# Second layer's first product by Strassen's seven block products over 768 tokens, its d_ff sums in SBUF, its weights unpacked early to DRAM

## The chip, the cores and the metric

The kernel runs on one core of one Trainium2 chip. The core has a matmul engine (TensorE: PE, and PEld for its weight loads), VectorE (DVE), ScalarE (ACT), GpSimd (POOL) and SyncE (SP), which here issues the DMAs. Each engine takes its instructions in the order written for it; semaphores hold it where it needs another's result. The metric is the device time of one execution in microseconds.

## The reference, cut to what matters

```python
x = attention(q, k, v, f)             # 4 x 8 x 576 x 64, causal with decay -> 2304 tokens x 512
h = x @ w_in                          # layer 1: 512 -> 2048
g = s * np.maximum(h, 0.0) ** 2 + b
x = g @ w_out                         # 2048 -> 512
h = x @ w_in                          # layer 2, other weights: 512 -> 2048
g = np.maximum(h, 0.0) + alpha * np.minimum(h, 0.0)
return g @ w_out                      # 2048 -> 512, float32
```

## The kernel before

**Number format.** Each factor of a product is split into two parts of reduced precision, `hi` and `lo = x - hi`, and each product takes three passes (hi·hi, lo·hi, hi·lo, the tuple `PASSES`). So a block product of 512 (d_model) by 128 (d_ff) by 512 tokens is 4 × 3 = 12 matmuls of 512 columns.

**Who sets the order.** Operations are put down as tasks (`task`) with a modelled cost, what they read and write, the ring buffers they use and a priority; a list scheduler in the kernel file writes each engine's instructions from these. A task offered for two engines goes where the model finishes it first. On the chip each engine then follows its list in order.

**Stages.** Attention writes x; beside it layer 1's first d_ff half runs over six blocks of 256 tokens. From about 398 us on come the remaining tokens (groups `67` and `8`, 512 and 256 tokens) and then layer 1's second half for the groups p0, p1 and p2 of 512 tokens. Layer 2 follows at 597 us over groups of 512, 512, 512, 512 and 256 tokens (`order = [3, 0, 1, 2, 4]`).

**One step of layer 2** (`moe_step` with `moe` 2), for one chunk `fc` of 128 of the 2048 d_ff: the first product `t_mm1` (L851, 12 matmuls into a PSUM bank of ring h or k); ACT scales it by alpha (L858); DVE takes the larger of that and the plain value (L864); ACT casts to `hi` (L868); DVE subtracts to `lo` (L879); the second product `t_mm2` (L886, 12 matmuls, each 512 output columns wide) adds into four PSUM banks of rings a and b, which sum over all 16 chunks. `finish_out` then copies the four banks to SBUF (L982) and stores them.

**Between the layers.** `finish_x1` adds layer 1's first-half sums, kept in DRAM (`pa_d`), to the banks of its second half (L953), splits the result into hi and lo, and stores it (`x1_d`); `load_x` brings it back.

**Weights.** They come as 64-bit words. `convert` loads one 128 × 512 block (512 KB, `raw`), scales words on ACT (L426), puts them together in three DVE operations (L417, L420, L423; the last two read both `raw` and the half-made `cv`), then casts to hi on ACT and takes lo on POOL (L443; for `wo2` on DVE, L441). Layer 2's are converted partly during layer 1, partly after it has begun.

## Time and profile before

| | before |
|---|---|
| time, median of 3 runs | 1008.03 us |
| runs | 1007.60, 1008.03, 1010.24 us |
| span of the profiled execution | 1006.3 us |
| its own time | not listed apart from the runs |
| busy share of PE, DVE, ACT, POOL | 99%, 55%, 45%, 23% |

The span runs from the first to the last instruction that the profile shows. An engine's busy time is the sum of its instructions' durations, register, branch and DMA-issuing ones left out; PE's matmuls overlap a little at their ends, so that the pace of a run of equal matmuls (start to start) is shorter than the listed mean of one.

### The profile page before, as it was taken

How to read it: one execution, taken by the hardware profiler on the slowest of the kernel's cores; microseconds unless marked ns; L12 is line 12 of the kernel's file. 1: busy time of each engine (PE TensorE's matmuls, PEld its weight loads, DVE VectorE, ACT ScalarE, POOL GpSimd, SP SyncE). 2: the span in 40 equal slices, each digit the busy share in tenths (PEclk: the TensorE clock that was granted, in tenths of full speed). 3: DMA queues.
4: the chain of work that ended last, by engine and by line, in shares of the span. 5: the costliest groups of instructions: out<-in, count | busy, mean ns of one | idle time of the engine just before them, and what ended most of it. 6: DMA issues, size and time to landing. Idle time of an engine off the chain costs nothing.

```text
span 1006.3 us, 15579 instructions
## 1 busy us (share of the span) xinstructions
PE 996.9 (99%) x5691; PEld 835.1 (83%) x5691; DVE 554.0 (55%) x1262; ACT 450.7 (45%) x1067; POOL 234.1 (23%) x275
## 2 busy tenths in 40 slices
...
GB/s 221 234 191 171 139 110 210 83 104 131 136 116 31 189 142 131 138 132 259 100 172 68 219 224 175 1 0 126 1 1 84 42 1 0 84 1 1 1 42 21
DMA packets 45519, 106.45 MB, mean 106 GB/s; under 512 B 4492, under 2 KB 23524, under 8 KB 44516
## 3 DMA queue, kind: packets, MB, share of 16 engines
...
q8 instruction: 45, 0.74, 0.3%
...
## 4 chain that ended last, share of the span: by engine, by line
PE 96%; DVE 1%; ACT 1%; issue 0%; DMA 0%; POOL 0%; SPq 0%; POOLq 0%; ACTq 0%
PE h L851 24%; PE k L851 16%; PE b L886 11%; PE a L888 9%; PE b L891 9%; PE a L886 9%; PE t L802 5%; PE t L749 4%; PE a L891 2%; PE s L674 2%; PE s L675 2%; PE s L679 2%; PE h L392 1%; DMA ft<-in_f_dram 0%; DVE cv L423 0%
## 5 line engine op out<-in xcount | busy, mean ns | idle before, releaser
L851 PE MATMUL h<-x,i 128*128 128x256 f32 (+1 forms) x1344 | 256.6, 340 | 0.6 <-DVE r L862 0.6
L851 PEld LDWEIGHTS h<-x,i 128*128 128x128 f32 x1344 | 210.9, 189 | 32.3 <-DVE r L862 1.9
L851 PE MATMUL k<-x,i 128*128 128x512 f32 (+1 forms) x672 | 153.4, 377 | 0.0
L851 PEld LDWEIGHTS k<-x,i 128*128 128x128 f32 x672 | 120.7, 188 | 25.5
L886 PE MATMUL b<-o,g 128*128 128x512 f32 x480 | 121.1, 393 | 0.0
L879 DVE TENSOR_TENSOR g<-r,g 128x512 fp32r<-128x512 f32 (+1 forms) x80 | 51.1, 638 | 120.9 <-ACT g L868 120.9
L709 POOL TENSOR_SCALAR e<-e,rec 128x128 f32<-128x128 f32 (+4 forms) x144 | 88.7, 627 | 86.1 <-DVE rec L702 35.7
L886 PEld LDWEIGHTS b<-o,g 128*128 128x128 f32 x480 | 90.2, 188 | 20.5
L868 ACT CAST g<-r 128x512 fp32r<-128x512 f32 (+1 forms) x78 | 45.1, 578 | 137.1 <-PE b L886 87.2
L888 PE MATMUL a<-g,o 128*128 128x256 f32 x768 | 104.5, 285 | 0.0
L443 POOL TENSOR_TENSOR i<-cv,i 128x512 fp32r<-128x512 f32 x32 | 47.7, 1490 | 243.5 <-ACT i L433 235.8
L886 PE MATMUL a<-o,g 128*128 128x512 f32 x384 | 98.8, 393 | 0.0
L888 PEld LDWEIGHTS a<-g,o 128*128 128x128 f32 x768 | 96.8, 190 | 1.2 <-issue 0.7
L891 PE MATMUL b<-g,o 128*128 128x512 f32 x384 | 95.3, 394 | 0.0
L877 DVE SCALAR_TENSOR_TENSOR g<-r,small,g 128x256 fp32r<-128x256 f32 (+1 forms) x104 | 70.1, 674 | 41.4 <-ACT g L870 40.7
L698 ACT ACTIVATE e<-e,ngm 128x128 f32<-128x128 f32 (+4 forms) x144 | 84.2, 586 | 14.8 <-DVE ngm L693 12.9
L891 PEld LDWEIGHTS b<-g,o 128*128 128x128 f32 x384 | 72.0, 188 | 16.8
L886 PEld LDWEIGHTS a<-o,g 128*128 128x128 f32 x384 | 71.1, 188 | 15.1
L870 ACT ACTIVATE g<-r,small 128x256 fp32r<-128x256 f32 (+1 forms) x90 | 53.2, 591 | 59.9 <-PE b L891 30.1
L693 DVE CUSTOM_DVE_ANT_0 e<-s,mask 128x128 f32<-128x128 f32 (+4 forms) x144 | 67.1, 480 | 16.9 <-PE s L675 7.8
L749 PE MATMUL t<-ident,e 128*128 128x128 f32 (+1 forms) x400 | 65.4, 276 | 3.5 <-ACT pt L758 2.1
L864 DVE SCALAR_TENSOR_TENSOR r<-k,sg_t,r 128x512 f32<-128x512 f32 (+1 forms) x40 | 27.9, 697 | 73.3 <-ACT r L858 73.3
...
## 6 DMA issues: line engine op xcount, KB each, us to landing
...
```

Of the source, the lines that this page charges most:

```text
L693: nc.vector.tensor_tensor_reduce(e.t[0:rows, k0:k1], st_.t[0:rows, 0:w], mask[0:rows, m0:m0 + w], -0.125 if u.f32 else -1.0, init, ALU.add ...
L698: nc.scalar.activation(x, x, AF.Exp, bias=ng[0:rows, col:col + 1], scale=-1.0, accum_out=sm[0:rows, col:col + 1])
L709: eng.tensor_scalar(x, x, rc[0:rows, col:col + 1], 1.0, ALU.mult, ALU.mult)
L749: nc.tensor.transpose(pp.t[0:kw, i * P:i * P + P], e.t[:, P * kb:P * kb + kw], ident)
L802: nc.tensor.matmul(o.t[64 * j:64 * j + 64, a - q0:z - q0], vb.t[0:kr, kb, j, :], uu.pt[jj].t[0:kr, kb * PTS + a:kb * PTS + z], start=(i == ...
L851: nc.tensor.matmul(ps.t[:, 0:w], wv[:, wl, kc, :], x.t[:, kc, xl, x0:x0 + w], start=(n == 0), stop=(n == 3 * KC - 1))
L870: eng.activation(g.t[:, 0, 0:w], r.t[:, 0:w], AF.Identity, bias=b_t)
L877: nc.vector.scalar_tensor_tensor(g.t[:, 1, 0:w], r.t[:, 0:w], b_t, h, ALU.add, ALU.subtract)
L879: nc.vector.tensor_tensor(g.t[:, 1, 0:w], r.t[:, 0:w], h, ALU.subtract)
L886: nc.tensor.matmul(acc[u].t, g.t[:, gl, u * P:u * P + P], wo.t[:, wl, :], start=(first and i == 0), stop=end)
L888: nc.tensor.matmul(acc[u // 2].t[:, T * (u % 2):T * (u % 2) + T], wo.t[:, wl, u * P:u * P + P], g.t[:, gl, 0:w], start=(first and i == 0 a ...
L891: nc.tensor.matmul(acc[u].t[:, 0:w], wo.t[:, wl, u * P:u * P + P], g.t[:, gl, 0:w], start=(first and i == 0), stop=end)
```

## The change

**First product.** Layer 2 goes over three groups of 768 tokens, and takes d_ff in eight pairs of chunks. For a pair, W (512 × 256) and x (512 × 768) are seen as 2 × 2 blocks (d_model halves by d_ff chunks, d_model halves by token halves). Winograd's form of Strassen's scheme gives the four 128 × 384 result blocks from seven block products of 256 × 128 by 384 tokens in place of eight. Each is 2 × 3 matmuls of 384 columns (L1096 of the new file). The table `PRODUCTS` names for each the weight operand, the token operand and the bank (Z, X, Y, W: one bank each of rings h and k, two of ring a); the last three add onto a product already there. Between them ACT copies two banks to SBUF (`s1`, `s5`, L1108) and DVE makes the sums (`u2`, `u3`, `c12`, `c21`, L1111, L1140; six of the 24 `u3` sums with two SBUF operands of the first group's pairs are POOL's, L1141).

**Gates.** Each of the four blocks gets the operations of before, on 384 columns (ACT L1124, DVE L1126, cast L1128, `lo` L1130).

**Second product and its sums.** Six tiles `y` of 128 tokens, each six matmuls of 512 columns over the pair's two chunks (L1162), in ring b of four banks; DVE adds each to a sum in SBUF (L1171; the first pair of a group copies, L1168), stored after the last pair.

**Token operands.** `finish_x2` takes the place of `finish_x1`: it makes the seven token operands of the scheme out of x's four blocks, with hi and lo of each, on DVE and ACT, through a ring `so` of four buffers, and stores them in 84 pieces (`x2_d`).

**Weights.** `keep` unpacks all 32 blocks of `wi2` and `wo2` during layer 1, and stores the unpacked float32 (`w2f_d`). `sums_of`, in the first group, makes four sums of weight blocks and hi and lo of all seven operands of a pair (on DVE, ACT and POOL), and stores them (`w2i_d`, 1.835 MB a pair), from where the other two groups load them (each group takes the pairs in the opposite direction to the one before, and its first two pairs' operands are still there); `outs_of` makes hi and lo of `wo2` for every pair and group anew. Pools for these (`w2`, `px`) open as layer 1's weights are done with. Attention and layer 1's first half keep their operations.

```diff
-    open_pool("wA", side="left")
+    open_pool("wA", side="right")
...
-    x1_d = [dram.tile([P, KC, 2, T2 if n < 4 else T], F32R, name=f"x1_d{n}") for n in range(5)]
+    x2_d = [dram.tile([P, 7, 2, 2, TH], F32R, name=f"x2_d{n}") for n in range(3)]
+    w2i_d = [dram.tile([P, 7, 2, T], F32R, name=f"w2i_d{n}") for n in range(NP2)]
+    w2f_d = {(key, n): dram.tile([P, 512], F32, name=f"{key}f_d{n}") for key in ("wi2", "wo2") for n in range(NF)}
...
+        "wi2": ring("w2", "wi2", 2, [P, 7, 2, T], F32R),
+        "wo2": ring("w2", "wo2", 2, [P, 2, 2, 512], F32R),
+        "cf": ring("w2", "cf", 4, [P, 512], F32),
+        "so": ring("w2", "so", 4, [P, 2 * T], F32),
+        "sw": ring("w2", "sw", 1, [P, 4, T], F32),
+        "y": ring("psc", "b", 4, [P, 512], F32),
+        "gq": ring("px", "gq", 8, [P, 2, TH], F32R),
+        "rt": ring("px", "rt", 2, [P, TH], F32),
...
+    def keep(key, fc, prio):
+        cv = R["cv"].buf()
+        K = unpack(key, fc, prio, cv)
+        task(("sp", kb_of(P * 2048), lambda: load(w2f_d[key, fc], cv.t.bitcast(F32))), r=[(K, "v")], w=[(K, "f")], bufs=[cv], prio=prio)
+
+    def fetch(key, fc, tag, prio):
+        c = R["cf"].buf()
+        K = (tag, key, fc)
+        task(("sp", kb_of(P * 2048), lambda: load(c.t, w2f_d[key, fc])), r=[((key, fc), "f"), "w2"], w=[K], bufs=[c], prio=prio)
+        return c, K
+
+    def sums_of(p, tag, prio):
...
+        both(T, [k1], [S[0]], [c1, sw], lambda e: e.tensor_tensor(s_of(0), part(c1, 0), part(c1, 1), ALU.add))
+        both(T, [k0, k1], [S[2]], [c0, c1, sw], lambda e: e.tensor_tensor(s_of(2), part(c0, 0), part(c1, 0), ALU.subtract))
+        both(T, [k0, S[0]], [S[1]], [c0, sw], lambda e: e.tensor_tensor(s_of(1), s_of(0), part(c0, 0), ALU.subtract))
+        both(T, [k0, S[1]], [S[3]], [c0, sw], lambda e: e.tensor_tensor(s_of(3), part(c0, 1), s_of(1), ALU.subtract))
+        done = []
...
+            task([("act", act(n, False), lambda a=a, z=z, src=src: nc.scalar.copy(wi.t[:, a:z, 0, :], src())),
+                  ("dvp", dve2(n), lambda a=a, z=z, src=src: nc.vector.tensor_copy(wi.t[:, a:z, 0, :], src()))], r=r, w=[hk], bufs=bufs + [wi], prio=prio)
+            both(n, r + [hk], [lk], bufs + [wi],
+                 lambda e, a=a, z=z, src=src: e.tensor_tensor(wi.t[:, a:z, 1, :], src(), wi.t[:, a:z, 0, :].bitcast(F32), ALU.subtract))
+            done += [hk, lk]
+        task(("sp", kb_of(P * 14336), lambda: rdma(w2i_d[p], wi.t)), r=done, w=[("w2i", p)], bufs=[wi], prio=prio)
+        return wi, done
...
+                def split(op, e, h, k=k, blk=blk, s0=s0, hw=hw, d0=d0, f=f, fk=fk, piece=piece):
...
+                    task(("sp", kb_of(P * 8 * hw), lambda: rdma(x2_d[blk][:, op, k, :, d0:d0 + hw], o2())), r=[(K, "hi"), (K, "lo")],
+                         w=[("x2d", blk, op, k, d0)], bufs=[st_], prio=epr)
...
+                split(0, 0, 0)
+                less(0, 0, 0, 1, 0, 0)
+                split(3, 0, 0)
+                split(2, 1, 1)
+                less(0, 1, 1, 1, 0, 1)
+                split(5, 0, 1)
+                less(1, 1, 1, 1, 0, 0)
+                split(4, 1, 1)
+                split(1, 1, 0)
+                less(1, 0, 1, 0, 1, 1)
+                split(6, 1, 0)
...
+    PRODUCTS = ((0, 0, "Z", True), (3, 3, "X", True), (5, 5, "Y", True), (4, 4, "W", True),
+                (1, 1, "Z", False), (6, 2, "X", False), (2, 6, "Y", False))
...
+                    if n == 0:
+                        wi, ki = sums_of(p, n, z - 8)
+                    else:
+                        wi, ki = R["wi2"].buf(), [("w2il", n, p)]
+                        task(("sp", kb_of(P * 14336), lambda wi=wi, p=p: rdma(wi.t, w2i_d[p])), r=[("w2i", p)], w=ki, bufs=[wi], prio=z - 6)
+                    wo, ko = outs_of(p, n, z - 6)
...
+        def product(i):
+            wop, xo, bk, start = PRODUCTS[i]
+            xb, view, slot = xop[xo]
...
+                for k in range(2):
+                    for wl, xl in PASSES:
+                        nc.tensor.matmul(b.t[:, 0:TH], wi.t[:, wop, wl, k * P:k * P + P], x[:, k, xl, :], start=(start and m == 0), stop=(m == 5),
+                                         skip_group_check=True)
...
+        for i in range(4):
+            product(i)
+            if i == 0:
+                copy("s1", "Z")
+            if i == 1:
+                copy("s5", "X")
+        add("u2", "W", "s1")
+        add("u3", "Y", "u2")
+        task([("dvp", dve(TH), lambda: nc.vector.tensor_tensor(t("u3"), t("u3"), t("s5"), ALU.add)),
+              ("pool", pool2(TH), lambda: nc.gpsimd.tensor_tensor(t("u3"), t("u3"), t("s5"), ALU.add))], r=[("t", "s5")], w=[("t", "u3")],
+             bufs=[tmp["u3"], tmp["s5"]], prio=epr)
+        gate(1, 1, src="u3")
+        product(4)
+        gate(0, 0, bankname="Z")
+        product(5)
+        add("c12", "X", "u2")
+        gate(0, 1, src="c12")
+        product(6)
+        add("c21", "Y", "u2")
+        gate(1, 0, src="c21")
+        for h in (1, 0):
+            for j in range(3):
+                u = 3 * h + j
+                y = R["y"].buf()
+                YK = (K, "y", u)
+
+                def go(h=h, j=j, y=y):
+                    m = 0
+                    for e in range(2):
+                        for gl, wl in ((0, 0), (0, 1), (1, 0)):
+                            nc.tensor.matmul(y.t, G[e, h].t[:, gl, j * P:j * P + P], wo.t[:, e, wl, :], start=(m == 0), stop=(m == 5))
+                            m += 1
+                task(("pe", 6 * MM[512], go), r=ko + [((K, e, h), x) for e in range(2) for x in ("hi", "lo")], w=[YK], bufs=[G[0, h], G[1, h], wo, y],
+                     prio=z + 2.9 + 0.01 * u)
+                if first:
+                    Y[u] = R["o"].buf()
+                    task([("act", act(512), lambda o=Y[u], y=y: nc.scalar.copy(o.t, y.t)), ("dve", dve(512), lambda o=Y[u], y=y: nc.vector.tensor_copy(o.t, y.t))],
+                         r=[YK], w=[("Y", n, u)], bufs=[y, Y[u]], prio=epr + 1)
+                else:
+                    task(("dve", dve(512), lambda o=Y[u], y=y: nc.vector.tensor_tensor(o.t, y.t, o.t, ALU.add)), r=[YK], w=[("Y", n, u)], bufs=[y, Y[u]],
+                         prio=epr + 1)
+                if last:
+                    row = rows[u]
...
+    second_layer([(0, rows(1536, 2048)), (1, rows(0, 512)), (2, rows(1024, 768))], pos[0] + 4.0, EPR)
```

**PE at the turn from layer 1 to layer 2.** Before, the last second products of layer 1 (L891, three matmuls into each of the four banks `b_8` to `b_11`) stand between first products of layer 2's first chunks; h, k and a are PSUM rings, `x_7` the tokens, `i..` and `o..` weight tiles.

```order
L891 MATMUL b_11_6836<-g2_54_7044,o6_0_5359 128x512 x3
L851 MATMUL k_28_7120<-x_7_6676,i1_1_5579 128x512 x12
L891 MATMUL b_8_6833<-g2_55_7092,o7_0_5458 128x512 x3
L891 MATMUL b_9_6834<-g2_55_7092,o7_0_5458 128x512 x3
L891 MATMUL b_10_6835<-g2_55_7092,o7_0_5458 128x512 x3
L891 MATMUL b_11_6836<-g2_55_7092,o7_0_5458 128x512 x3
L851 MATMUL h_78_7163<-x_7_6676,i2_1_5662 128x512 x12
L851 MATMUL k_29_7196<-x_7_6676,i3_1_5728 128x512 x12
L886 MATMUL a_18_7224<-o0_1_5540,g2_56_7133 128x512 x3
L886 MATMUL a_19_7225<-o0_1_5540,g2_56_7133 128x512 x3
L886 MATMUL b_12_7226<-o0_1_5540,g2_56_7133 128x512 x3
L886 MATMUL b_13_7227<-o0_1_5540,g2_56_7133 128x512 x3
```

After it, layer 1's last products stand together, and seven products of the first pair (weights `wi2_0`) follow, then those of the second pair (`wi2_1`) among them.

```order
L942 MATMUL b_8_7023<-g2_55_7376,o7_0_5496 128x512 x3
L942 MATMUL b_9_7024<-g2_55_7376,o7_0_5496 128x512 x3
L942 MATMUL b_10_7025<-g2_55_7376,o7_0_5496 128x512 x3
L942 MATMUL b_11_7026<-g2_55_7376,o7_0_5496 128x512 x3
L1096 MATMUL h_77_7411<-x_7_6913,wi2_0_5622 128x384 x6
L1096 MATMUL k_28_7430<-x_7_6913,wi2_0_5622 128x384 x6
L1096 MATMUL a_18_7441<-xs_1_6596,wi2_0_5622 128x384 x6
L1096 MATMUL a_19_7451<-x_8_7351,wi2_0_5622 128x384 x6
L1096 MATMUL h_77_7411<-x_8_7351,wi2_0_5622 128x384 x6
L1096 MATMUL a_19_7451<-x_8_7351,wi2_1_5853 128x384 x6
L1096 MATMUL k_28_7430<-xe0_0_7425,wi2_0_5622 128x384 x6
L1096 MATMUL h_77_7411<-x_7_6913,wi2_1_5853 128x384 x6
```

First products of layer 2 no longer stand ahead of layer 1's last second product; the fourth product of the second pair needs the bank `a_19` that the first pair's sum reads.

**DVE at the same place.** Before, the sums of layer 1's last group (L953 out of banks `b_8` to `b_11`, L956 for `lo`) stand among the gates of layer 2's first chunks (L864, L879).

```order
L879 TENSOR_TENSOR g2_57_7176<-r2_57_7151,g2_57_7176 128x512
L966 CAST o_54_7194<-o_54_7194 128x256
L864 SCALAR_TENSOR_TENSOR r2_58_7211<-h_78_7163,sg_t_96,r2_58_7211 128x512
L956 TENSOR_TENSOR o_54_7194<-o_54_7194 128x256
L953 TENSOR_TENSOR o_56_7219<-b_10_6835,o_52_7182 128x256
L441 SCALAR_TENSOR_TENSOR o5_1_7161<-cv_59_7137,sg_t_96,o5_1_7161 128x512
L956 TENSOR_TENSOR o_56_7219<-o_56_7219 128x256
L953 TENSOR_TENSOR o_57_7243<-b_10_6835,o_52_7182 128x256
L864 SCALAR_TENSOR_TENSOR r2_59_7240<-k_29_7196,sg_t_96,r2_59_7240 128x512
L956 TENSOR_TENSOR o_57_7243<-o_57_7243 128x256
L953 TENSOR_TENSOR o_58_7249<-b_11_6836,o_55_7213 128x256
```

After it, the same banks are read by L989, x's operands (`so`, ring of four) are made from them, and then come the sums of the first pair (`u2`, `u3`) and its gates (`rt`).

```order
L989 TENSOR_TENSOR o_28_7201<-b_9_7024,o_28_7201 128x512
L989 TENSOR_TENSOR o_29_7208<-b_11_7026,o_29_7208 128x512
L1010 TENSOR_TENSOR so_70_7428<-o_26_6853,so_70_7428 128x256
L1017 TENSOR_TENSOR o_26_6853<-o_26_6853 128x256
L1008 CAST so_72_7462<-o_27_6858 128x256
L1017 TENSOR_TENSOR o_26_6853<-o_27_6858,o_26_6853 128x256
L1010 TENSOR_TENSOR so_71_7460<-o_26_6853,so_71_7460 128x256
L1010 TENSOR_TENSOR so_72_7462<-o_27_6858,so_72_7462 128x256
L1010 TENSOR_TENSOR so_73_7474<-o_26_6853,so_73_7474 128x256
L1017 TENSOR_TENSOR o_27_6858<-o_27_6858,o_26_6853 128x256
L1111 TENSOR_TENSOR u2_0_7479<-a_19_7451,s1_0_7437 128x384
L1111 TENSOR_TENSOR u3_0_7487<-a_18_7441,u2_0_7479 128x384
```

The sums `u2` and `u3` of the first pair stand behind layer 1's last sums, and eight operations on x's operands are between.

**SP between the first and second group of 768.** The rows are DMAs: `w2i_d5`, `w2i_d6` and so on are the DRAM copies of pairs' operands, `cf` the tiles into which unpacked blocks of `w2f_d` are loaded, `x2_d1` and `x2_d2` the token operands of the second and third group. No such rows stood before at that place.

```order
L320 DMA w2i_d7_98<-wi2_7_8365 128x3584
L320 DMA x_7_6913<-x2_d1_89 128x1536 x2
L320 DMA xs_1_6596<-x2_d1_89 128x1536
L320 DMA x_8_7351<-x2_d2_90 128x1536 x2
L320 DMA xe0_0_7425<-x2_d2_90 128x1536
L320 DMA xe1_0_7465<-x2_d2_90 128x1536
L317 DMA wo2f_d15_130<-cv_63_8375 128x512
L320 DMA wi2_8_8661<-w2i_d5_96 128x3584
L317 DMA cf_31_8722<-wo2f_d15_130 128x512
L317 DMA cf_32_8725<-wo2f_d10_125 128x512
L317 DMA cf_33_8737<-wo2f_d11_126 128x512
```

The last block of `wo2` is stored (`wo2f_d15`) behind the loads of the second group's tokens, and is loaded again (`cf_31`) behind the first reload of weights, `wi2_8`.

## Rows read from the trace of the kernel before

**Rows 1.** Page of the profile: busy time of each engine, and shares of the last-ending chain
```profile
span 1006.3 us, 15579 instructions
PE 996.9 (99%) x5691; PEld 835.1 (83%) x5691; DVE 554.0 (55%) x1262; ACT 450.7 (45%) x1067; POOL 234.1 (23%) x275
...
PE 96%; DVE 1%; ACT 1%; issue 0%; DMA 0%; POOL 0%; SPq 0%; POOLq 0%; ACTq 0%
```

**Rows 2.** Windows: length, busy (count) by engine, granted clock, DMA share, GB/s
```profile
13.00:23.00 10.00, 9.65 (x52) 6.92 (x51) 6.66 (x28) 6.21 (x19) 6.10 (x7) 0.74 0.76 241
...
350.00:475.00 125.00, 125.00 (x727) 110.21 (x726) 108.65 (x172) 67.37 (x124) 35.61 (x22) 1.00 0.47 154
460.00:468.00 8.00, 8.00 (x48) 7.00 (x46) 6.27 (x11) 3.41 (x6) 1.29 (x1) 1.00 0.95 342
602.90:1002.50 399.60, 399.56 (x1825) 329.30 (x1823) 129.46 (x205) 109.30 (x183) 3.01 (x2) 1.00 0.10 36
```

**Rows 3.** Timeline of PE in layer 2: start, duration, matmuls, and their number
```profile
597.30 2.93 PE L851 MATMUL h<-x,i 128*128 128x512 f32 x12
...
968.36 1.60 PE L851 MATMUL k<-x,i 128*128 128x256 f32 x12
969.80 1.55 PE L886 MATMUL a<-o,g 128*128 128x512 f32 x6
...
998.08 4.38 PE L886 MATMUL a<-o,g 128*128 128x512 f32 x18
```

**Rows 4.** Lines by form, DVE, whole span: busy us, mean ns, idle before
```profile
L879 DVE TENSOR_TENSOR g<-r,g 128x512 fp32r<-128x512 f32 x64 | 44.3, 692 | 107.8 <-ACT g L868 107.8
L417 DVE TENSOR_SCALAR cv<-raw 128x512 int32<-128x512 int32 x64 | 31.5, 492 | 13.2 <-ACT raw L426 12.1 <-issue 0.4
L864 DVE SCALAR_TENSOR_TENSOR r<-h,sg_t,r 128x512 f32<-128x512 f32 x32 | 24.0, 751 | 63.5 <-ACT r L858 63.5
...
L879 DVE TENSOR_TENSOR g<-r,g 128x256 fp32r<-128x256 f32 x16 | 6.8, 425 | 13.1 <-ACT g L868 13.1
L953 DVE TENSOR_TENSOR o<-b,o 128x256 f32<-128x256 f32 x16 | 6.1, 418 | 0.2 <-DMA o<-pa_d 0.2
...
L864 DVE SCALAR_TENSOR_TENSOR r<-h,sg_t,r 128x256 f32<-128x256 f32 x8 | 3.9, 484 | 8.5 <-ACT r L858 8.5
L982 DVE COPY o<-b 128x512 f32<-128x512 f32 x5 | 3.4, 688 | 1.1 <-PE b L886 1.1
```

**Rows 5.** Lines by form, DVE, 475 to 550 us
```profile
L877 DVE SCALAR_TENSOR_TENSOR g<-r,small,g 128x512 fp32r<-128x512 f32 x14 | 10.5, 751 | 22.5 <-ACT g L870 22.5
L423 DVE SCALAR_TENSOR_TENSOR cv<-raw,cv 128x512 int32<-128x512 int32 x2 | 1.4, 686 | 0.0
L420 DVE SCALAR_TENSOR_TENSOR cv<-raw,cv 128x512 int32<-128x512 int32 x2 | 1.4, 681 | 0.0
```

**Rows 6.** Timeline of POOL and DVE near 380 us
```profile
379.92 1.81 POOL L443 TENSOR_TENSOR o<-cv,o 128x512 fp32r<-128x512 f32 x1 [2.60 <-ACT o L433]
380.61 1.68 DVE L423 SCALAR_TENSOR_TENSOR cv<-raw,cv 128x512 int32<-128x512 int32 x1
...
383.01 1.29 POOL L443 TENSOR_TENSOR i<-cv,i 128x512 fp32r<-128x512 f32 x1 [1.29 <-ACT i L433]
```

**Rows 7.** Lines by form, DVE, 350 to 475 us
```profile
L420 DVE SCALAR_TENSOR_TENSOR cv<-raw,cv 128x512 int32<-128x512 int32 x30 | 26.0, 868 | 0.5
L423 DVE SCALAR_TENSOR_TENSOR cv<-raw,cv 128x512 int32<-128x512 int32 x30 | 25.7, 857 | 0.2
L877 DVE SCALAR_TENSOR_TENSOR g<-r,small,g 128x512 fp32r<-128x512 f32 x14 | 11.7, 836 | 1.7 <-ACT g L870 1.6
L877 DVE SCALAR_TENSOR_TENSOR g<-r,small,g 128x256 fp32r<-128x256 f32 x16 | 10.6, 660 | 1.1 <-ACT g L870 0.9
```

**Rows 8.** One load of a raw weight block, timeline: its issue, and the first reader
```profile
584.74 0.33 SPq L315 DMA_DIRECT2D raw<-in_wi_dram  x1
...
588.27 0.67 ACT L426 ACTIVATE raw<-raw 128x512 f32<-128x512 f32 x1 [1.25 <-DMA raw<-in_wi_dram]
```

More of the change, by code (lines that the diff above doesn't have):

```diff
@@ L31 @@
 T2 = 2 * T
+TH = 384
+NP2 = NF // 2
 NB = NT // T
@@ L875, in t_d @@
             h = g.t[:, 0, 0:w].bitcast(F32)
-            if moe == 1:
-                nc.vector.scalar_tensor_tensor(g.t[:, 1, 0:w], r.t[:, 0:w], b_t, h, ALU.add, ALU.subtract)
-            else:
-                nc.vector.tensor_tensor(g.t[:, 1, 0:w], r.t[:, 0:w], h, ALU.subtract)
+            nc.vector.scalar_tensor_tensor(g.t[:, 1, 0:w], r.t[:, 0:w], b_t, h, ALU.add, ALU.subtract)
         def t_mm2():
-            for u in range(KC if moe == 1 else w // P):
+            for u in range(KC):
                 for i, (wl, gl) in enumerate(PASSES):
                     end = last and i == 2
-                    if moe == 2:
-                        nc.tensor.matmul(acc[u].t, g.t[:, gl, u * P:u * P + P], wo.t[:, wl, :], start=(first and i == 0), stop=end)
-                    elif len(acc) == 2:
+                    if len(acc) == 2:
                         nc.tensor.matmul(acc[u // 2].t[:, T * (u % 2):T * (u % 2) + T], wo.t[:, wl, u * P:u * P + P], g.t[:, gl, 0:w],
@@ L1054, in to_b @@
         close_pool("pg")
-        open_pool("wB", side="right", reuse_waits="tile")
         open_pool("pg2", side="left", reuse_waits="tile")
+        open_pool("wB", side="left", reuse_waits="tile")
         open_pool("psc", space=PSUM, reuse_waits="tile")
@@ L1064, in decay_attention_two_moe, with step @@
     cnt = [0]
-    def step(moe, name, fc, x, w, xk, acc, first, last):
+    def step(name, fc, x, w, xk, acc, first, last):
         p = pos[0]
-        AK = moe_step(moe, name, fc, x, 0, w, xk + ["wB"], acc, "hk"[cnt[0] % 2], first, last, p, p + 2.5, EPR, True)
+        AK = moe_step(name, fc, x, 0, w, xk + ["wB"], acc, "hk"[cnt[0] % 2], first, last, p, p + 2.5, EPR, True)
         cnt[0] += 1
@@ L1079, in decay_attention_two_moe, with to_c @@
     keys = {}
+    n0 = len(sc.tasks)
     for n, (name, x, w, xk, acc) in enumerate(three):
         for fc in lo_f:
-            step(1, name, fc, x, w, xk, acc, fc == 0, False)
+            step(name, fc, x, w, xk, acc, fc == 0, False)
+    def to_c():
+        close_pool("wA")
+        open_pool("w2", side="right", reuse_waits="tile")
+    task(("py", 0.0, to_c), r=["wB"], started=sc.tasks[n0:], w=["w2"])
     xl = {}
-    xl[1, 0] = load_x(1, 0, EPR)
-    for fc in range(HF):
+    xl[0] = load_x(0, EPR)
@@ L1087, in decay_attention_two_moe @@
+    for p in range(NP2):
         for key in ("wi2", "wo2"):
-            convert(key, fc, 1100.0 + 4 * fc)
+            for e in range(2):
+                keep(key, 2 * p + e, 1100.0 + 8 * p)
+    n0 = len(sc.tasks)
     for fc in hi_f:
         for name, x, w, xk, acc in three:
-            keys[name] = step(1, name, fc, x, w, xk, acc, False, fc == NF - 1)
-    for n, (name, x, w, xk, acc) in zip((3, 4), three):
-        finish_x1(n, [6, 7] if n == 3 else [8], acc, keys[name], EPR, False)
+            keys[name] = step(name, fc, x, w, xk, acc, False, fc == NF - 1)
```

337 lines of the change are left out of this document (197 added, 140 removed).

## The prediction

> **What bounds the kernel now.** The page comes first: PE is busy for 996.9 of 1006.3 us, and it holds 96% of the chain that ended last [rows 1]. Then the windows by stage: from 602.90 to 1002.50 us PE is busy for 399.56 of 399.60 us, at full granted clock, while DVE is busy for 129.46, ACT for 109.30 and POOL for 3.01 us, at a DMA share of 0.10 [rows 2]. Layer 2 is bound by its count of matmul columns, and the other engines have room. Last the timeline, which gives the pace of one matmul from start to start [rows 3]. So fewer columns shorten the span by what they cost, as long as operations that weren't there before don't make PE wait. Where they are dense, layer 1's end and the first group of 768, is the question.
>
> **What the first product saves.** A first product of 256 columns takes (969.80 − 968.36)/12 = 0.120 us a matmul [rows 3]. Layer 2 runs from 597.30 to 998.08 + 4.38 = 1002.46, 405.16 us. In it the program has 192 matmuls of 256 columns and 1656 of 512: 768 of the first product, 864 of the second and 24 left over from layer 1. So one of 512 takes (405.16 − 192 × 0.120)/1656 = 0.2308 us. None has 384 columns here; the straight line between gives 0.1752 (bounds: three quarters of 0.2308 = 0.1731, one and a half of 0.1195 = 0.1793). The first product of before took 768 × 0.2308 + 192 × 0.1195 = 200.2 us; the new one has 24 pairs × 42 = 1008 of 384 columns, 176.6 us. **Saved: 23.6 us** (19.5 to 25.7). The second product keeps its 864 matmuls. A pair now gives PE 42 × 0.1752 + 36 × 0.2308 = 15.67 us.
>
> **DVE in the second and third group.** Prices [rows 4]: two SBUF operands 0.692 us at 512 columns and 0.425 at 256, so 0.56 at 384; the gate from PSUM 0.751 and 0.484, so 0.617; PSUM plus SBUF 0.418 at 256, and 0.688, that of the copy, at 512, so 0.55. The `lo` of `wo2` is taken at 0.751 [rows 5]. A pair has four PSUM sums (2.2), one `u3` sum (0.56), four gates (2.47), four `lo` (2.24), six sums of `y` (4.1) and two `lo` of `wo2` (1.5): 13.1 of 15.67 us. PE stays the bound there, and the third group's last sum (0.69) takes the place of the copy at the end: nothing to add.
>
> **The turn from layer 1 to layer 2.** Layer 1's last sums (L989, four of 0.69) can't start before its last second product ends. Behind them on DVE stand eight operations at 256 columns on x's operands, seven of them with two operands (0.425), some 3.3 us, then `u2` (0.55): it is done 6.6 us after that end. PE has five products of 6 × 0.1752 = 1.05 us meanwhile; the sixth, the fourth product of the second pair, needs the bank that `u2` reads and waits 1.3 us. Two products later Z is needed, which its gate leaves 2.8 us after `u2` (0.55, 0.56, 0.42, 0.62, 0.62): 0.7 more. That is 2.0 us even if DVE comes to the turn on time. From p2's first gate to `u2` DVE has 50.4 us of operations by these prices, PE 51.3 (17 groups of 12 × 0.2308, four products). In the earlier stretch where it was as dense, 350 to 475 us, DVE was idle for 125.00 − 108.65 = 16.35 us, 13%, behind waits [rows 2]. Half to all of that share on 50.4 us is 3.3 to 6.6, less 0.9 of slack: 2.4 to 5.7 more. **I take +4**, the lower of these with the 2.0, rounded down (2 to 8).
>
> **The first group of 768: DVE beside POOL.** Pairs 2 to 7 have 132 DVE operations there (25 PSUM sums, 24 gates, 26 two-operand sums at 384 columns, 36 sums of `y`, 4 at 256, 11 `lo` of `wo2`, 6 of the last unpacking at 0.49, 0.68 and 0.69): 81.6 us, 13.6 a pair. POOL has 17,920 columns in them, at 1.29 us per 512 (its fastest) 45 us, 7.5 a pair [rows 6]. While POOL works on two SBUF operands, DVE's operations of that kind stretch: L423 took 1.68 us from 380.61 with POOL at work from 379.92 for 1.81 [rows 6], and 0.686 where POOL was idle, like L420's 0.681 [rows 5]. How much in all: in 350 to 475 us L420 and L423 lost 30 × (868 − 681) and 30 × (857 − 681), L877 14 × (836 − 751) ns, 12.1 us, and if its 256-wide form is priced by L864's 484, 16 × (660 − 484) more, 14.9 [rows 4, 5, 7]. POOL was busy for 35.61 us [rows 2]. So 0.34 to 0.42 of POOL's time came back on DVE. At 0.42 a pair costs DVE 13.6 + 3.15 = 16.75 us against PE's 15.67: 1.08 × 6 = 6.5 us late; at 0.34, 0.48 × 6 = 2.9. **I take +4.5**, between these (0 to 33, the latter at all of POOL's time: (13.6 + 7.5 − 15.67) × 6).
>
> The Trainium skill, "GPSIMD Engine Reference", section "1. Specifications", says that POOL's SBUF interfaces are shared with VectorE and contend with VectorE instructions that have two SBUF inputs. The row at 380.61 agrees. Read as shutting DVE out for POOL's whole time, it would give 13.6 + 7.5 = 21.1 us a pair; the measured share gives 16.75, since part of DVE's work reads PSUM.
>
> **Between the first and second group.** The second group begins with the last two pairs' weights still in place. The first reload (`wi2_8`, 1.835 MB) can start only when its first pair is through its products, and the last `wo2` block, which the first group's last `y` tiles need, stands behind it on SP. At 342 GB/s [rows 2] the reload takes 5.4 us, and the fixed part of a load is about 2.0: 512 KB took 3.5 us from 584.74 to 588.27 [rows 8], 1.5 of them at 342 GB/s. With the block's hi and lo (ACT some 0.7 as the row at 588.27, DVE 0.75) that is 9 to 10 us, against the next pair's products and three more, 7.36 + 3 × 1.05 = 10.5. Hidden when all is on time; **I take +1** (0 to 3).
>
> **Moved without cost.** Unpacking stays three DVE operations a block; it moves from layer 2, where DVE idles, to 430 to 600 us. The casts of `wo2` recur three times, on ACT at under half busy.
>
> **The sum.** −23.6 + 4 + 4.5 + 1 = −14.1 on the profiled 1006.3 us: 992.2. The median is 1.7 us above that span, what lies around it included, so **994 us**.
>
> **Rivals.**
> *Nearly all of the saving comes through.* DVE and POOL run ahead in the unevenness of pairs and the turn costs its 2.0 us: 986, between 984 and 990. For it: 13.1 of 15.67 us in the steady groups. Against: POOL's share. Chance 0.20.
> *POOL's time falls on DVE.* The first group has more two-operand work than 350 to 475 us. The loss in the first group must be 23.6 − 4 − 1 = 18.6 us to cancel the gain, 3.1 a pair: a share of (15.67 + 3.1 − 13.6)/7.5 = 0.69. A share of 0.6 gives 1004, one of 1 gives 1022. Against it stand 0.34 to 0.42. Chance 0.11. The rule of the page named above, taken whole, is the end at 1.
> *The DMA queue is the bound from the unpacking to the end of the first group.* By the tile sizes in the listing 67.6 MB move while PE has 256 us of work: 264 GB/s. 342 at a share of 0.95 is the most that rows show [rows 2], but 84 stores of x's operands (16.5 MB) go in rows of 1 KB and 512 bytes, and 220 to 241 GB/s at 0.74 to 0.76 early in the span [rows 2] make some 300 at best. Below 67.6 MB/(256 + 23.6 us) = 242 GB/s the saving is gone; at 230 the time is 1022. Chance 0.10.
> *PE's clock falls in the first pairs of the first group*, when waits break up its work. In 13 to 23 us the granted clock was 0.74, with PE busy 9.65 of 10 us on small matmuls [rows 2]. Three pairs are 47 us: at 0.74 they cost 47 × 0.35 = 16.5 us more, 1010. For it: waits between short products. Against: 1.00 in every later window. Chance 0.07.
> The change does its work in any case: 1008 matmuls of 384 columns stand in the listing.
>
> **How the numbers follow.** The forecast, 990 to 1003 about 994, keeps 0.52. A change under 0.3% (1005 to 1011) is about what a measurement of this kernel can't tell from none. Faster: 0.52 + 0.20 + 0.02 of POOL's case and 0.02 of the clock's, 0.76; same: 0.03 + 0.02 + 0.03 = 0.08; slower: 0.06 + 0.08 + 0.02 = 0.16. The range goes from 984, the saving with the turn's least cost, to 1009, which leaves out most of the slower cases: 984 to 1009.
>
> **What the profile will show.** Matmuls of 384 columns at 0.173 to 0.179 us from start to start; pairs of the second and third group at 15.7 us with PE idle near nothing; at the turn, PE waiting for `u2` and for the gate on Z, together 2 to 6 us; in the first group DVE's `lo` above 0.56 us and PE's waits on DVE; POOL's sums about 45 us. I am wrong if PE waits there for DMAs (`x2_d`, `cf`), if its granted clock falls below 1.00, or if 384 columns cost more than 0.18.

## The result, and the profile after

| | before | changed |
|---|---|---|
| median | 1009.13 us | 995.18 us |
| runs, lowest to highest | 1007.6 to 1011.42 (4) | 993.26 to 995.76 (4) |
| ratio | | 0.9855, 95% interval 0.9835 to 0.9874 |
| span of the profiled execution | 1006.3 us | 993.0 us |

The forecast was 994 us, between 984 and 1009. The total came out within 1.2 us; two terms of its sum were off by more than that.

The page of the changed kernel: busy times, and the shares of the chain of work that ended last.

```profile
span 993.0 us, 16601 instructions
PE 976.1 (98%) x5739; PEld 844.7 (85%) x5739; DVE 745.8 (75%) x1668; ACT 509.1 (51%) x1224; POOL 277.6 (28%) x319
...
PE 82%; DMA 7%; DVE 6%; ACT 2%; issue 1%; SPq 1%; POOL 1%; ACTq 0%; POOLq 0%; DVEq 0%
```

Beside [rows 1] PE lost 20.8 us of work and DVE gained 192; PE is still busy for 98% of the span. The windows (columns as in [rows 2]) show where it isn't: the turn and the first pairs, 600 to 650 us. Later it is dense.

```profile
600.00:650.00 50.00, 46.65 (x231) 40.74 (x230) 44.07 (x83) 29.05 (x62) 15.64 (x13) 1.00 0.93 322
602.00:728.00 126.00, 121.41 (x596) 107.28 (x595) 114.80 (x188) 66.40 (x133) 51.83 (x45) 1.00 0.72 259
760.00:860.00 100.00, 100.00 (x495) 89.69 (x494) 73.12 (x130) 39.37 (x73) 0.00 (x0) 1.00 0.37 129
```

PE's waits from 560 us on, in groups (us in total, times, longest). What released PE was DVE or ACT each time, never a DMA; but a DMA can stand behind these, as the chain's 7% says, and at the turn one does (below).

```profile
PE h L1096 <- DVE rt L1126: 1.7, 2, 1.5
PE a L1096 <- DVE u L1111: 1.5, 2, 1.3
PE b L1162 <- DVE o L1171: 1.2, 1, 1.2
PE b L942 <- ACT g L926: 1.1, 1, 1.1
```

The timeline of PE (start, us) at the turn and, below, over one pair of the second group, which answers to [rows 3]:

```profile
598.80 3.37 PE L942 MATMUL b<-g,o 128*128 128x512 f32 x12 [1.09 <-ACT g L926]
602.01 1.22 PE L1096 MATMUL h<-x,wi 128*128 128x384 f32 x6
...
608.79 1.32 PE L1096 MATMUL a<-x,wi 128*128 128x384 f32 x6 [1.32 <-DVE u L1111]
610.06 1.29 PE L1096 MATMUL k<-xe,wi 128*128 128x384 f32 x6
612.89 1.32 PE L1096 MATMUL h<-x,wi 128*128 128x384 f32 x6 [1.53 <-DVE rt L1126]
...
806.32 1.22 PE L1096 MATMUL h<-xe,wi 128*128 128x384 f32 x6
807.38 1.22 PE L1096 MATMUL k<-xe,wi 128*128 128x384 f32 x6
...
813.74 8.59 PE L1162 MATMUL b<-wo,gq 128*128 128x512 f32 x36
```

The next pair starts at 822.17: a pair takes 15.85 us, the first product (813.74 − 806.32)/42 = 0.1767 a matmul, the second (822.17 − 813.74)/36 = 0.2342. Layer 2 runs from 602.01 to its last matmul's end at 989.24 (972.20 + 17.04), 387.2 us. So the 13.3 us between the spans split up thus: layer 1 ends 0.9 us earlier (597.30 + 24 × 0.2333 = 602.9 before, without layer 2's interleaved products); 24 pairs of 15.85 are 380.4 in place of 399.6 us, **−19.2**; waits, and slower matmuls right behind them, **+6.8**; the end stays at 3.8 us.

### The profile page after: what moved, and what is told of

It reads as the page before. It is cut to its first block, busy times and chain, and to the rows that moved or that the text cites. A ratio compares the mean times of both kernels' runs of the same rounds, so it can differ in the third digit from the quotient of the medians.

```text
span 993.0 us, 16601 instructions
## 1 busy us (share of the span) xinstructions
PE 976.1 (98%) x5739; PEld 844.7 (85%) x5739; DVE 745.8 (75%) x1668; ACT 509.1 (51%) x1224; POOL 277.6 (28%) x319
## 4 chain that ended last, share of the span: by engine, by line
PE 82%; DMA 7%; DVE 6%; ACT 2%; issue 1%; SPq 1%; POOL 1%; ACTq 0%; POOLq 0%; DVEq 0%
PE b L1162 18%; PE h L915 12%; PE a L939 9%; PE a L1096 7%; PE b L942 6%; PE t L866 5%; PE k L915 5%; PE h L1096 4%; PE t L813 4%; PE k L1096 4%; DMA raw<-in_wo_dram 3%; PE s L738 2%; DMA x_d<-so 2%; PE s L739 2%; PE s L743 2%
## 5 line engine op out<-in xcount | busy, mean ns | idle before, releaser
L1162 PE MATMUL b<-wo,gq 128*128 128x512 f32 x864 | 208.2, 397 | 1.4 <-DVE o L1171 1.2
L1162 PEld LDWEIGHTS b<-wo,gq 128*128 128x128 f32 x864 | 162.1, 188 | 38.5 <-DVE o L1171 1.6
L915 PE MATMUL h<-x,i 128*128 128x256 f32 (+1 forms) x864 | 149.2, 321 | 0.6 <-DVE r L922 0.6
L915 PEld LDWEIGHTS h<-x,i 128*128 128x128 f32 x864 | 126.2, 188 | 13.9 <-DVE r L922 1.7
L1171 DVE TENSOR_TENSOR o<-b,o 128x512 f32<-128x512 f32 x126 | 84.1, 683 | 26.5 <-PE b L1162 26.5
L922 DVE SCALAR_TENSOR_TENSOR r<-h,small,r 128x256 f32<-128x256 f32 (+1 forms) x76 | 42.8, 563 | 35.9 <-ACT r L919 35.6
L824 ACT COPY pt<-t 128x256 f32<-128x256 f32 (+2 forms) x128 | 55.1, 451 | 20.4 <-PE t L813 19.9
L441 ACT ACTIVATE raw<-raw 128x512 f32<-128x512 f32 x64 | 43.4, 678 | 41.0 <-DMA raw<-in_wo_dram 21.1
L813 PEld LDWEIGHTS t<-ident,e 128*128 128x128 f32 (+1 forms) x400 | 46.6, 139 | 15.6 <-issue 8.0
L1128 ACT CAST gq<-rt 128x384 fp32r<-128x384 f32 x91 | 46.5, 513 | 21.7 <-DVE rt L1126 16.2
```

Source lines behind the costliest of these rows:

```text
L813: nc.tensor.transpose(pp.t[0:kw, i * P:i * P + P], e.t[:, P * kb:P * kb + kw], ident)
L824: copy(x.t[0:kw, a:a + PTS * m].rearrange("p (m w) -> p m w", w=PTS)[:, :, 0:w], src)
L915: nc.tensor.matmul(ps.t[:, 0:w], wv[:, wl, kc, :], x.t[:, kc, xl, x0:x0 + w], start=(n == 0), stop=(n == 3 * KC - 1))
L1162: nc.tensor.matmul(y.t, G[e, h].t[:, gl, j * P:j * P + P], wo.t[:, e, wl, :], start=(m == 0), stop=(m == 5))
L1171: task(("dve", dve(512), lambda o=Y[u], y=y: nc.vector.tensor_tensor(o.t, y.t, o.t, ALU.add)), r=[YK], w=[("Y", n, u)], bufs=[y, Y[u]], pr ...
```

## The experiments

All are compared with the kernel before, timed beside them, by their ratio (95% interval); times are medians of 4 to 6 runs. "Pace" is the time from start to start of a matmul in a run of equal ones.

**The changed kernel again.** 

> The changed kernel itself, once more, as the measure for the other kernels timed beside it. Expected: 994 to 996 us; the pair of the second and third group at 15.85 us as in its first trace (42 matmuls of 384 columns at 0.1767, 36 of 512 at 0.2342). If the two paces that 512-wide matmuls show in the traces (0.2267 and 0.2333) are a matter of the tiles, they stand at the same places again; if they are a state of the chip in that execution, they stand elsewhere.

994.53 us, 0.9868 (0.9846 to 0.9890). The paces stood at the same places again: 0.2333 at 340 us, 0.2267 at 480, 0.1767 and 0.2342 in layer 2. They belong to the tiles. In the built program, in bytes of a partition, layer 1's first-half weights moved from 17,472 to 163,808 and its second-half weights from 163,808 to 95,296; layer 2's lie at 172,000 and above. Matmuls with weights from 163,808 on are slow, in both kernels.

One thing differs from the first trace. PE waited 1.87 us for `u2` in place of 1.32, and behind that wait the granted clock was at its lower level of 1.2 GHz for most of 4 us (means of 0.60 and 0.55 in two windows); six matmuls of 384 columns took 2.26 us in place of 1.29:

```profile
608.00:610.00 2.00, 1.87 (x8) 1.39 (x7) 0.75 (x2) 0.00 (x0) 0.00 (x0) 0.60 0.91 282
610.00:612.00 2.00, 1.74 (x6) 1.23 (x4) 1.32 (x3) 1.64 (x4) 0.00 (x0) 0.55 0.99 363
```

So the rival of the clock is met in the changed kernel itself, for a short stretch. Much of its cost was hidden: the next wait, for the gate on Z, was 0.56 us in place of 1.53.

**32 bytes lower on the right side.**

```diff
+    open_pool("pad", side="right"); pools["pad"][0].tile([P, 8], F32, name="pad")
     open_pool("wA", side="right")
```

> The only edit: an unused tile of 32 bytes is allocated first on the right side of SBUF, so that every tile of the right side (layer 2's weights, and those of layer 1's first half) starts 32 bytes lower, at a multiple of 64. Theory one, a weight tile that starts 32 bytes past a multiple of 64 costs PE about 7 ns a 512-wide matmul: the second product goes from 0.2342 to 0.227 (864 x 0.007 = 6 us), the first from 0.1767 to about 0.173 (1008 x 0.0034 = 3.4 us), layer 1's 192 of 512 columns on that side from 0.2333 to 0.2267 (1.3 us): 984 to 986 us. Theory two, tiles high up in SBUF are slow whatever their alignment: nothing moves, 994 to 996. Theory three, the pace is a state of the execution: no fixed answer.

992.55 us, 0.9842 (0.9826 to 0.9858), not clearly apart from the changed kernel. The paces stayed near the slow ones (36 of the second product from 812.31 to 820.68, 8.37 us, 0.2325 each). Theory one, in this form, falls.

**416 bytes lower.**

```diff
-    open_pool("pad", side="right"); pools["pad"][0].tile([P, 8], F32, name="pad")
+    open_pool("pad", side="right"); pools["pad"][0].tile([P, 104], F32, name="pad")
```

> As with the 32 bytes, but 416 bytes lower, so that the weights of the right side start at 64 past a multiple of 512, as all tiles of the left side do (where 512-wide matmuls went at 0.2267). Theory one (the start of the weights modulo 512 sets the pace): the second product at 0.227 and the first near 0.173, 984 to 986 us. Theory two (how high the weights lie in SBUF): no change against the 32 bytes, 0.2333 and 0.176, 992 to 995.

986.15 us, **0.9786 (0.9763 to 0.9808)**: theory one. One pair in its timeline:

```profile
808.58 8.36 PE L1162 MATMUL b<-wo,gq 128*128 128x512 f32 x36
816.78 1.23 PE L1096 MATMUL h<-xe,wi 128*128 128x384 f32 x6
817.85 1.20 PE L1096 MATMUL k<-xe,wi 128*128 128x384 f32 x6
818.89 2.24 PE L1096 MATMUL a<-xe,wi 128*128 128x384 f32 x12
...
824.09 8.36 PE L1162 MATMUL b<-wo,gq 128*128 128x512 f32 x36
```

From 808.58 to 824.09 are 15.51 us, 0.34 less than before the shift, × 24 = 8.2 us, which is the gain. The second product goes at 8.20/36 = 0.2278, the first at (818.89 − 817.85)/6 = 0.1733, with nothing moved but the right side's tiles, by 384 bytes against the run with 32.

**All pools on the other side.** Each `side="left"` becomes `side="right"`, and the other way round.

```diff
-    open_pool("const", side="left")
-    open_pool("wA", side="right")
+    open_pool("const", side="right")
+    open_pool("wA", side="left")
...
```

> Every pool changes sides: what was allocated from the bottom of SBUF is now allocated from the top, and the other way round. Layer 2's weights lie at 24,704 to 73,856, x's own tiles above 162,848, the x operands and gates of layer 2 between. Theory two (weights high up are slow): the second product goes to 0.2267 in every group, and so does layer 1's 340 to 372 stretch; its later half may go to 0.2333 only if x or its weights there count; 986 to 989 us. If any high operand is slow, the first product stays at 0.1767 for the x operands that lie in x's own tiles and falls for the others. Rival (the place in SBUF has no part): the old paces at the old places in the program, 993 to 996 us.

990.73 us, 0.9821 (0.9801 to 0.9842). Layer 2's weights lie low now, and its second product still takes 0.2333:

```profile
811.25 8.56 PE L1162 MATMUL b<-wo,gq 128*128 128x512 f32 x36
819.65 1.22 PE L1096 MATMUL h<-xe,wi 128*128 128x384 f32 x6
```

So height falls as the cause. Layer 1's second half, with weights and x both at 32 past a multiple of 256, keeps 0.2267. Layer 2's first product goes at 0.1733 in one pair and 0.1767 in the next, which I can't explain.

**160 bytes, and a fifth tile for x's operands.** 

```diff
+    open_pool("pad", side="right"); pools["pad"][0].tile([P, 40], F32, name="pad")
...
-        "so": ring("w2", "so", 4, [P, 2 * T], F32),
+        "so": ring("w2", "so", 5, [P, 2 * T], F32),
```

> Two edits whose effects show at different places. First, 160 unused bytes on the right side, so that the weights there start at 64 past a multiple of 256, but at 320 past one of 512; the tiles of the left side start at 64 past a multiple of 512. If the start modulo 256 sets the pace of 512-wide matmuls, 0.2267 to 0.228 in the second product, as with 416 bytes; if it is modulo 512, 0.2333. Second, the ring of tiles through which x's operands are stored has five tiles in place of four. If the wait for the gate on Z at the turn (1.5 us in the changed kernel) comes from DVE standing in order behind an x operand that waits for its tile's store, it falls below 0.6 us; if it comes from the count of DVE operations, it stays above 0.7. Time: 985 to 988 with the fast pace, 992 to 995 without.

988.07 us, 0.9793 (0.9772 to 0.9814). The pace is the fast one, 8.20/36 = 0.2278:

```profile
814.17 8.36 PE L1162 MATMUL b<-wo,gq 128*128 128x512 f32 x36
822.37 1.23 PE L1096 MATMUL h<-xe,wi 128*128 128x384 f32 x6
```

So 256 is enough as a modulus. The starts in the built programs, modulo 256, and the paces of layer 2:

| kernel | weights | x and gates | second product | first product |
|---|---|---|---|---|
| changed | 224 | 64 | 0.2342 | 0.1767 |
| 32 bytes | 192 | 64 | 0.2325 | 0.176 |
| 416 or 160 bytes | 64 | 64 | 0.2278 | 0.1733 |
| sides exchanged | 128 | 32 | 0.2333 | 0.1733 and 0.1767 |

In these kernels the pace is fast where the two starts agree modulo 256, and slow where they differ by 96, 128 or 160, but for the last kernel's first product, which was both. Other differences were not tried, and why the chip does so is not shown. The second half of the expectation failed:

```profile
617.12 2.29 PE L1096 MATMUL h<-x,wi 128*128 128x384 f32 x6 [3.52 <-DVE rt L1126]
```

The gate on Z held PE for 3.52 us in place of 1.53, and the granted clock was 0.50 to 0.52 behind it, from 616 to 622 us. But the scheduler had also moved the gate behind more of x's operands, with POOL's `u3` sum ahead of it. What a fifth tile alone does stays open.

**The kernel before, 416 bytes lower on the right side.**

```diff
     open_pool("const", side="left")
+    open_pool("pad", side="right"); pools["pad"][0].tile([P, 104], F32, name="pad")
     open_pool("wA", side="left")
```

> The kernel before, with the same 416 unused bytes first on the right side, where the second half of its weights lies. By the theory of the start modulo 512, its 512-wide matmuls with those weights go from 0.2333 to 0.2267: 768 in layer 1 and 768 in layer 2, 10 us, so 998 to 1000 us; the changed kernel's gain over it, both shifted, would then be some 12 to 14 us. If the pace there has another cause: 1008 to 1010.

998.79 us, 0.9883 (0.9863 to 0.9903), as expected: 11.2 us under the kernel before timed beside it (1010.01). The changed kernel with 416 bytes is 22.7 us under the one beside it (1008.88). So with both kernels shifted the change brings some 11.5 us (12.6 if the two medians are compared directly, though they come from separate timings); without the shift it brought 14.0 and, in the second timing, 14.8. The slow pace costs the kernel before 11 us and the changed kernel some 8, a difference that the intervals leave open.

**One product issued twice.**

```diff
+        product(0)
         for i in range(4):
             product(i)
```

> The first of the seven products of each pair is issued twice (the second starts its sum anew, so the output stays): 48 matmuls of 384 columns a pair, as many columns as a plain product would need, in the changed kernel's staging. Theory one (PE's columns set the time): 24 x 1.06 = 25.4 us more than without the edit, less the few us of waits that the extra work hides: 1017 to 1021, 8 to 12 us above the kernel before, which is then the price of the new staging. Rival (another engine or the DMA queue has become the bound of layer 2's first group): about a third of the 25 us is hidden, 1010 to 1013.

1017.72 us, 1.0089 (1.0075 to 1.0104): 23.2 us over the changed kernel, of 25.4 issued, as theory one has it. Leaving out the eighth product saves almost all that its columns cost, and the new staging with the old number of columns costs 8.4 us against the kernel before, its slower tiles included.

**x's last operands after the first gates.** `finish_x2` leaves the operands of p2 to a function that the first pair calls behind its gates; each of its operations also reads the gate on Z.

```diff
+        if name != "p2":
+            return splits()
+        later.append(splits)
...
         gate(1, 0, src="c21")
+        if later:
+            later.pop()([((K, 0, 0), "r")])
```

> The operands of x that layer 1's last group leaves are made after the first pair's gate on Z, in place of ahead of u2. Theory one (the turn's waits come from the eight operations between layer 1's last sums and u2): PE's waits for u2 (1.3 us) and for the gate on Z (1.5 us) go, with the slow matmuls behind them some 3 us, unless the operands of x then push later pairs: 991 to 993. Rival (DVE is behind at the turn in any case, and the same work only moves): the waits come back one or two pairs on, same time as without the edit within 1 us.

1003.63 us, 0.9942 (0.9925 to 0.9959): 9 us slower than without the edit, which neither theory gave. The two waits at the turn went, as theory one has it (one of 1.25 us for the load of an x operand, now late, came there), and what came later was more than they: timeline of PE, and windows of two of these stretches.

```profile
635.65 0.73 PE L1169 MATMUL b<-wo,gq 128*128 128x512 f32 x2 [0.92 <-ACT gq L1133]
638.12 2.39 PE L1169 MATMUL b<-wo,gq 128*128 128x512 f32 x6 [1.73 <-DVE gq L1135]
...
684.42 2.93 PE L1169 MATMUL b<-wo,gq 128*128 128x512 f32 x6 [4.55 <-DVE o L1178]
```

```profile
635.00:637.00 2.00, 0.73 (x2) 0.30 (x2) 2.00 (x2) 1.04 (x4) 2.00 (x2) 1.00 0.86 278
639.00:641.00 2.00, 2.00 (x6) 1.61 (x5) 2.00 (x7) 0.02 (x1) 0.11 (x1) 0.50 1.12 459
```

DVE is full in both windows. Work that is pushed from the turn into the first group is added to an engine without room, and holds PE at the gates and at the sums of `y`. Behind the two waits, 0.92 + 1.73 = 2.65 us, the granted clock was 0.50, its lower level of 1.2 GHz, and six matmuls took 2.39 us. The same came behind the wait of 4.55 us: 0.50 from 684 to 690 us. So the rival of the clock is met here twice, for longer than in the changed kernel.

**The weight sums on DVE alone.**

```diff
-            task([("dvp", dve(n), lambda: f(nc.vector)), ("pool", pool2(n), lambda: f(nc.gpsimd))], r=r, w=w, bufs=bufs, prio=prio)
+            task(("dvp", dve(n), lambda: f(nc.vector)), r=r, w=w, bufs=bufs, prio=prio)
```

> The sums and low parts of layer 2's weights in the first group are made on DVE alone, none on POOL (the six u3 sums may still go there). Theory one (POOL gives DVE back about 0.35 of its own time as longer two-operand work, and DVE has some 1 us of room over six pairs): DVE gets 46 us / 1.29 x 0.69 = some 24 us more and loses some 15 us of stretching, so the first group is some 6 to 9 us longer, 1000 to 1004 us. Rival (POOL's share of the port costs DVE as much as the work itself): no change, 993 to 996, or faster.

992.10 us, 0.9841 (0.9819 to 0.9862): not slower, which is the rival. The intervals of this kernel and of the changed one overlap. The window that answers to the changed kernel's second one above:

```profile
602.00:728.00 126.00, 121.91 (x597) 108.84 (x596) 111.73 (x221) 64.75 (x130) 4.57 (x4) 0.99 0.63 221
```

POOL works 47 us less, DVE has 33 operations more, and DVE is busy for 111.73 us in place of 114.80. The scheduler's help from POOL was worth nothing. PE still waits 4.7 us from 560 us on, but in other places: 2.1 us for a cast on DVE (L1128), 1.8 us for the load of an x operand. The lines of DVE by form, first of the changed kernel from 602 to 728 us, then of this one:

```profile
L1130 DVE TENSOR_TENSOR gq<-rt,gq 128x384 fp32r<-128x384 f32 x32 | 23.5, 757 | 1.3 <-ACT gq L1128 1.2
L1126 DVE SCALAR_TENSOR_TENSOR rt<-c,sg_t,rt 128x384 f32<-128x384 f32 x16 | 12.4, 798 | 0.0
L516 DVE SCALAR_TENSOR_TENSOR wo<-cf,sg_t,wo 128x512 fp32r<-128x512 f32 x11 | 10.5, 980 | 0.0
```

```profile
L1130 DVE TENSOR_TENSOR gq<-rt,gq 128x384 fp32r<-128x384 f32 x30 | 15.8, 550 | 0.1
L516 DVE SCALAR_TENSOR_TENSOR wo<-cf,sg_t,wo 128x512 fp32r<-128x512 f32 x12 | 9.7, 808 | 0.1
L1126 DVE SCALAR_TENSOR_TENSOR rt<-c,sg_t,rt 128x384 f32<-128x384 f32 x16 | 9.4, 611 | 0.2 <-ACT rt L1124 0.2
```

**The made weights stored twice.** 

```diff
         task(("sp", kb_of(P * 14336), lambda: rdma(w2i_d[p], wi.t)), r=done, w=[("w2i", p)], bufs=[wi], prio=prio)
+        task(("sp", kb_of(P * 14336), lambda: rdma(w2y_d[p], wi.t)), r=done, w=[("w2y", p)], bufs=[wi], prio=prio)
```

> The operands made from each pair's weights in the first group are stored twice, the second time to a tensor that nobody reads: 8 x 1.835 = 14.7 MB more between 600 and 720 us, some 43 us of the DMA engines at 342 GB/s. Theory one (DVE, and not the DMA queue, is nearest to holding PE in the first group): some of it is hidden, yet a weight buffer comes free 5 us later, up to 5 us more, 994 to 1000. Rival (the DMA queue holds PE there): 20 us or more, over 1013.

1017.32 us, 1.0085 (1.0065 to 1.0105): some 22.8 us more than the changed kernel, as the rival has it. PE's longest wait:

```profile
773.89 26.33 PE L1164 MATMUL b<-wo,gq 128*128 128x512 f32 x103 [9.53 <-ACT wo L516]
```

This is the place between the first and second group: the last `wo2` block is late, and PE stands. It shows how little room the queue has, not that it holds PE without the extra stores. The next run takes stores away.

**Only the first pair's weights stored.**

```diff
+        if p == 0:
             task(("sp", kb_of(P * 14336), lambda: rdma(w2i_d[p], wi.t)), r=done, w=[("w2i", p)], bufs=[wi], prio=prio)
...
-                        task(("sp", kb_of(P * 14336), lambda wi=wi, p=p: rdma(wi.t, w2i_d[p])), r=[("w2i", p)], w=ki, bufs=[wi], prio=z - 6)
+                        task(("sp", kb_of(P * 14336), lambda wi=wi, p=p: rdma(wi.t, w2i_d[0])), r=[("w2i", 0)], w=ki, bufs=[wi], prio=z - 6)
```

> Only the first pair's weight operands are stored in the first group, and the other two groups load these for every pair (so the first product of their other pairs takes wrong weights; the work is the same): 12.8 MB less between 600 and 720 us. Theory one (DVE holds PE at the turn and in the first group, and the DMA queue only nearly does): the waits of PE for DVE stay, 992 to 996. Rival (the DMA queue sets when x's operands and the unpacked blocks come, and through them when DVE is free): PE's waits in 600 to 730 us go, 988 to 991.

997.12 us, 0.9875 (0.9855 to 0.9895), no gain, and PE's waits are again for DVE and ACT, though not the same ones:

```profile
PE a L1097 <- DVE c L1112: 4.7, 1, 4.7
PE b L943 <- DVE g L933: 1.1, 1, 1.1
PE b L943 <- ACT g L927: 0.8, 1, 0.8
PE h L1097 <- DVE rt L1127: 0.5, 1, 0.5
```

The wait of 4.7 us is new: the scheduler had put the operations in another order here too. From 620 to 730 us the DMA share fell from 0.68 to 0.39, and PE was busy for 109.04 of 110 us in place of 108.26, at a granted clock of 0.98: beyond the turn the queue is not what holds PE, while with 14.7 MB more it would be. The turn itself is not tested by this run. The stores left out begin at 621.22 us in the changed kernel, and from 600 to 610 us the queue is as full as before (a share of 1.00 in both).

**416 bytes and the sums on DVE together.** Both edits as above.

> The 416 bytes on the right side together with the weight sums on DVE alone. If the two gains are apart from each other (the pace of PE's matmuls, and DVE freed of POOL's share of the port), they add up: 986 less some 2, 983 to 985 us. If PE, being faster by 0.45 us a pair, now waits for DVE in the first group, the second gain is lost: 986 to 988.

**982.26 us, 0.9727 (0.9706 to 0.9748)**, faster than both kernels. The gains add up: with the shift, the sums on DVE bring 986.15 − 982.26 = 3.9 us, with intervals apart (0.9763 to 0.9808 for the shift alone); without it the difference was 2.4, where the intervals overlap.

## Why the prediction was right, and where two errors met

**Fewer columns: right in kind, too large by 4.4 us.** The forecast was −23.6 us, the measured change −19.2. The step that failed is the price of one matmul: the 0.2308 us of one of 512 columns was a mean over two paces, 0.2267 and 0.2333 to 0.2342, by where the weights lie. The change moved all of layer 2's weights to slow starts: 0.2342 for the second product, which "keeps its 864 matmuls", is 2.9 us more, and 0.1767 in place of 0.1752 for the first product is 1.5 us more. The bounds, 0.1731 and 0.1793, held both paces. The runs with 416 and 160 bytes show that the place of the weights is the cause. The trace of before had both paces, for whoever takes PE's timeline within one group of layer 2, by which half of the weights is in use:

```profile
702.43 2.88 PE L851 MATMUL k<-x,i 128*128 128x512 f32 x12
705.15 1.52 PE L886 MATMUL b<-o,g 128*128 128x512 f32 x6
...
740.77 2.96 PE L851 MATMUL h<-x,i 128*128 128x512 f32 x12
743.57 1.57 PE L886 MATMUL b<-o,g 128*128 128x512 f32 x6
```

(705.15 − 702.43)/12 is 0.2267, (743.57 − 740.77)/12 is 0.2333. The same moved layer 1, for which the prediction had nothing: with its first-half weights on slow starts its second half begins 2.2 us later (400.07 us for 397.82; 1.0 of it stood before the first 512-wide matmul), and with those of the second half on fast starts it ends 0.9 us earlier.

**The turn: right, with one wait more, which goes back to the DMA queue.** `u2` was forecast 6.6 us after layer 1's last product (602.17), and ends at 608.73; PE was to wait 1.3 us for it and waited 1.32. The gate on Z was to cost 0.7 and cost 1.53. The rows of DVE and ACT there:

```profile
608.18 0.55 DVE L1111 TENSOR_TENSOR u<-a,s 128x384 f32<-128x384 f32 x1
608.77 0.56 DVE L1111 TENSOR_TENSOR u<-a,u 128x384 f32<-128x384 f32 x1
609.36 0.56 DVE L1140 TENSOR_TENSOR u<-u,s 128x384 f32<-128x384 f32 x1
610.74 0.41 ACT L1007 CAST so<-o 128x256 fp32r<-128x256 f32 x1 [3.26 <-DMA x_d<-so]
611.17 0.43 DVE L1010 TENSOR_TENSOR so<-o,so 128x256 fp32r<-128x256 f32 x1 [1.25 <-ACT so L1007]
```

An x operand stands on DVE ahead of the gate and waits 1.25 us for ACT, and ACT 3.26 us for a tile that is still being stored. I had counted the operation's 0.42 us and not its wait. The chain that ended last goes through this store, of 5.30 us:

```profile
605.34 5.30 DMA x_d<-so
...
610.74 0.41 ACT so L1007
```

The DMA share was 1.00 from 600 to 610 us. So at this one place the DMA queue had a part in a wait that the prediction gave to DVE alone. That a larger ring or an emptier queue removes it is not shown. With the 1.09 us at 598.80, where layer 1's last gate is late, and the slower matmuls behind each wait, the turn costs about 5 us; the forecast was 4.

**The first group: the share was right, the loss smaller.** By the rows of 602 to 728 us DVE lost 32 × (757 − 549) + 16 × (798 − 609) ns, 11 × (980 − 748) and some 7 us on other lines, about 19 us (549, 609 and 748 are the means of the same lines in 760 to 985 us), 0.37 of POOL's 51.83; the forecast was 0.34 to 0.42. The prices of DVE's operations were right too (0.549 and 0.609 at 384 columns, for 0.56 and 0.617). PE waited 1.6 us, some 2.9 with the slower matmuls behind the waits, where 4.5 were taken, which I put down to the two pairs that the eight gate tiles can hold; that was not tried. The rule of the Trainium skill ("GPSIMD Engine Reference", section "1. Specifications": SBUF interfaces shared with VectorE) agrees with these rows: L1130, which has two SBUF inputs, takes 757 ns with POOL at work and 550 without. Taken as POOL's whole time it would have been far off, since the share was 0.37. What the prediction lacked is the other half of this account: here POOL saved DVE no more than it took.

**Between the groups:** +1 was taken, and the list of waits has none there. **The end:** as forecast, 3.8 us on both sides.

So +4.4 on the products and −2.7 on all waits within layer 2 (6.8 for 9.5), and 0.9 won ahead of it, nearly cancel: 994 was met partly by luck. Of the rivals, the DMA queue held PE for long only under an edit that took its room away; in the changed kernel it had a part in the one wait at the turn. The clock stayed at 1.00 from 600 us to the last matmul in the changed kernel's first trace. In the second one it fell at the turn, so the sign "if its granted clock falls below 1.00" came true there, for some 3 us in place of the rival's three pairs, and the time stayed the same (994.53).
